# Attention scores in quarters of the TensorE array, in an attention and token-mixing kernel

## The chip, the cores and the metric

The kernel runs on one core of a Trainium2 chip. The metric is the device time of one execution in microseconds (us), as the median over runs. A core has TensorE (PE, matrix products into PSUM; its weight loads are listed apart as PEld), VectorE (DVE), ScalarE (ACT), GpSimd (POOL) and SyncE (SP), which run beside one another and wait for each other by semaphores.

## The reference

Attention with a local window and a few global keys, then a mixing layer on its output. Cut to what is computed:

```python
B, H, S, D = 4, 8, 768, 64;  n_global, n_local = 8, 96
scores = q @ k.T / sqrt(D)                        # per batch and head, 768 x 768
keep   = (key < n_global) | (0 <= query - key < n_local)
scores = where(keep, scores - slope[h] * dist, -1e9)   # dist: query - key, or n_local for global keys
a      = softmax(scores);   attn = a @ v
x      = attn with the heads side by side         # B, 768, 512
theta  = x @ w_theta
y      = w_tok_r @ (x * cos(theta)) + w_tok_i @ (x * sin(theta))
u      = x + y
out    = u + relu(u @ w_ch)                       # f32
```

## The kernel before

All matrix operands are bf16 and sums are f32. Queries and keys are cut into six tiles of 128 (T). Because the window is 96 and there are 8 global keys, a query tile needs its own key tile and the one before it; the first 8 keys of the earlier tile are replaced by the global ones in a second copy of the keys (`mT`, and `v_pv` for the values). Eleven blocks of 128 keys by 128 queries are left per head. They lie in three groups (`GROUPS`): group 0 with three blocks, groups 1 and 2 with four each. A group of two heads fills one `ps_w` tile of PSUM, two banks, one for each head; there are two such tiles.

Heads go in pairs (`h0` = 0, 2, 4, 6). `att_transpose` turns q and k of two heads so that the 64 channels lie in the partitions: head `h0` in partitions 0 to 63, head `h0 + 1` in 64 to 127. For batches 1 to 3 that is done by 48 transposes of 64 by 64 (L226), and two copies bring the result from PSUM to the tile `qk` (L232, both on ScalarE in the steps spoken of here). `att_scores` (L297) then makes one matmul per block and head: the stationary operand (weights) is a block of keys, 64 channels by 128 keys, in the upper or the lower half of the array's rows according to the head; the moving operand is the queries' 128 columns (256 where one key block serves two query tiles, in group 0). The weights of each matmul are loaded by an instruction of their own. ScalarE takes the exponential (L306), VectorE multiplies by a mask with the slopes in it (L317, L319), and `att_values` (L346) multiplies by the values, which also yields the sums of the softmax.

In batch 0 the bias is added in PSUM for groups 0 and 2: `att_bias` (L276) writes a product that covers the bank, and the scores add to it (L302 takes the exponential). In the other batches the scores start the sum themselves.

The program is written in the order in which each engine runs it (`K` keeps the program order). In batches 1 to 3 the attention of a batch runs beside the mixing of the batch before (`attend_beside`): for every two heads the order on PE is group 0's scores, some matmuls of the mixing (L430 with `w_tokT`, L472 with `w_ch`), the scores of groups 1 and 2, the transposes of the next two heads, more mixing, and the values. Between batches come the matmuls with `w_theta` (L395) with sine and cosine on ScalarE (L403, L404). Loads are issued by POOL, results and transposing DMAs by SP.

Of the kernel before, what the change touches and what calls it, by code (L numbers as in the profile page):

```python
# [16 lines left out]
def kernel(  # L17
# [13 lines left out]
    nc = tc.nc  # L31
    B, H, S, D = q.shape
    T = 128
# [20 lines left out]
    K = tc.keep_in_program_order  # L54

    def ps_wide():
        return psum.tile([T, 2, DM], FP, name="ps_w", tag="ps_w", bufs=2)
# [208 lines left out]
    def att_bias(h0, g_):  # L266

        ps = biased[h0, g_] = ps_wide()
        rows = dist.rearrange("a n t -> a (n t)")
        for hh in range(2):  # L270
            if g_ == 0:
                out_, rhs = ps[:, hh, 0:3 * T], rows
            else:
                out_ = ps[:, hh, :].rearrange("a (r x) -> a r x", r=2)
                rhs = rows[:, None, T:3 * T].to_broadcast([T, 2, 2 * T])
            K(nc.tensor.matmul(out_, lhsT=ident_d[:, h0 + hh, :], rhs=rhs,  # L276
                               start=True, stop=False))

    def att_scores(b, h0, g_, mul=True):
        qT, kT, mT = qTs[b, h0], kTs[b, h0], mTs[b, h0]  # L280
        blocks = GROUPS[g_]
        n = len(blocks)
        bias = b == 0 and g_ != 1
        if bias and (h0, g_) not in biased:
            att_bias(h0, g_)
        ps = biased[h0, g_] if bias else ps_wide()

        runs = [(0, 2)] + [(2, 1)] if g_ == 0 else [(i_, 1) for i_ in range(n)]
        for i_, w in runs:
            it, prev = blocks[i_]  # L290
            if prev == 0 or it == 1:
                keys = kT[:, (it - prev) * T:(it - prev + 1) * T]
            else:
                keys = mT[:, (it - 2) * T:(it - 1) * T]
            for hh in range(2):
                R = slice(D * hh, D * (hh + 1))
                K(nc.tensor.matmul(ps[:, hh, i_ * T:(i_ + w) * T],  # L297
                                   lhsT=keys[R, :], rhs=qT[R, it * T:(it + w) * T],
                                   start=not bias, stop=not bias or i_ == n - 1))
        if bias:  # L300
            p = abuf.tile([T, 2, 4 * T], BF, name="p", bufs=6)
            K(nc.scalar.activation(p[:, :, 0:n * T], ps[:, :, 0:n * T], AF.Exp, scale=scale))  # L302
            probs[b, h0, g_] = p
            return
        e = abuf.tile([T, 2, 4 * T], BF, name="e", bufs=3)
        K(nc.scalar.activation(e[:, :, 0:n * T], ps[:, :, 0:n * T], AF.Exp, scale=scale))  # L306
        exps[b, h0, g_] = e
        if mul:
            att_mul(b, h0, g_)

    def att_mul(b, h0, g_):
        e = exps[b, h0, g_]
        n = len(GROUPS[g_])
        p = abuf.tile([T, 2, 4 * T], BF, name="p", bufs=6)
        hs = slice(h0, h0 + 2)
        if g_ == 0:
            K(nc.vector.tensor_mul(p[:, :, 0:n * T], e[:, :, 0:n * T], wmask[:, hs, :]))  # L317
        else:
            K(nc.vector.tensor_mul(  # L319
                p.rearrange("a h (r x) -> a h r x", r=2),  # L320
                e.rearrange("a h (r x) -> a h r x", r=2),
                wmask[:, hs, None, T:3 * T].to_broadcast([T, 2, 2, 2 * T])))
        probs[b, h0, g_] = p
# [179 lines left out]
    def attend_beside(b, main, lead, load):  # L503


        def m(n=1):
            for _ in range(n):
                main.pop(0)()

        m(lead)  # L510
        for h0 in range(0, H, 2):
            att_scores(b, h0, 0)
            m(2 if h0 else 1)
            att_scores(b, h0, 1)
            att_scores(b, h0, 2)
            if h0 + 2 < H:
                att_transpose(b, h0 + 2, q_eng="act")
                if load and h0 == 0:
                    load_heads(b + 1, 0, 4)
                if load and h0 + 4 == H:  # L520
                    load_heads(b + 1, 4, 4)
                m(2)
            else:
                if load:
                    turn_x(b, NC - 2, False)
                m(len(main) - 1)
            att_values(b, h0)
            if h0 + 2 < H and not (load and h0 + 4 == H):
                turn_x(b, h0 // 2, True)
        m()  # L530
# [136 lines left out]
```

## Time and profile before

| | |
|---|---|
| Time, median of 3 runs | 171.58 us (171.09 to 172.12) |
| Profiled execution | 171.33 us, span 169.5 us |
| Granted TensorE clock | 1.000 |
| Busy: PE / PEld / DVE / ACT / POOL | 158.7 / 86.2 / 114.7 / 103.0 / 63.2 us |
| Score matmuls (L297) | 288 with 128 columns, 32 with 256 |
| Transposes in quarters (L226) | 576 |

The span is from the first to the last instruction of the program in one profiled execution; the time of the run is 1.8 us longer. A group's row gives the line, the engine, the operation with its output and inputs by name, the used rows*columns of the array (for PE), the shape and the count; then busy time, mean duration, and the idle time of the engine before it with what ended it. Matmuls overlap: one of 128 columns is listed with some 216 ns, while the next starts 56 ns later. So for PE the distances between starts tell more than durations. A few matmul records are missing from the trace (276 of 288 rows of L430 are there).

### The profile page before, as it was taken

The numbers are of one execution on the slowest core, as the hardware profiler recorded it, in microseconds if no ns is written. First come the engines' busy times: TensorE is split into PE (matmuls) and PEld (weight loads), VectorE is DVE, ScalarE is ACT, GpSimd is POOL, SyncE is SP. The second block draws the span as 40 slices with busy tenths as digits, with TensorE's granted clock in tenths as the row PEclk, the third lists the DMA queues.
The fourth block names the chain that finished last, engine by engine and source line by source line (L and its number), as shares of the span: only waits on it lengthen the run. The fifth ranks groups of instructions, "written<-read, shape, count | busy, mean of one in ns | idle before, by whom it ended". The sixth has DMA issues, their size and how long they took to land.

```text
span 169.5 us, 4624 instructions
## 1 busy us (share of the span) xinstructions
PE 158.7 (94%) x1965; PEld 86.2 (51%) x1988; DVE 114.7 (68%) x210; ACT 103.0 (61%) x120; POOL 63.2 (37%) x99
## 2 busy tenths in 40 slices
PE   7779999999899999999999999999999999999992
PEld 2346665555465654446555554445655544444440
DVE  7768875965858875767587694849568756534362
ACT  4989887957686562798658615996765618300010
POOL 8996797004484650032972900054245000000000
PEclk9999999999999999999999999999999999999999
DMA  4999999999999999910599999711953342121325
GB/s 148 194 180 190 209 211 208 198 180 182 158 140 196 141 173 215 257 70 4 92 145 170 155 187 197 210 62 37 73 110 95 99 148 86 68 60 34 113 102 186
DMA packets 57060, 24.08 MB, mean 142 GB/s; under 512 B 43088, under 2 KB 54096, under 8 KB 57040
## 3 DMA queue, kind: packets, MB, share of 16 engines
q0 software_dynamic: 35328, 12.45, 65.5%
q1 hardware_dynamic: 21440, 10.95, 31.2%
q10 hardware_dynamic: 272, 0.39, 0.7%
q8 instruction: 15, 0.25, 0.6%
q14 instruction: 5, 0.04, 0.1%
HBM read 25.69 MB, written 6.29 MB: 189 GB/s over the span
## 4 chain that ended last, share of the span: by engine, by line
PE 80%; DVE 6%; DMA 4%; issue 3%; POOL 3%; ACT 3%; DVEq 0%; ACTq 0%; POOLq 0%
PE ps_mm L430 35%; PE ps_mm L472 12%; PE ps_w L395 11%; PE ps_w L297 7%; PE ps_w L346 5%; DMA v_sb<-in_v_dram 4%; PE ps_tr L226 3%; PE ps_mm L346 2%; ACT e L306 2%; PE ps_tr L114 2%; DVE zri L411 1%; DVE w_tokT L117 1%; PE ps_tr L378 1%; DVE p L319 1%; ACT qk L249 1%
## 5 line engine op out<-in xcount | busy, mean ns | idle before, releaser
L430 PE MATMUL ps_mm<-zri,w_tokT 128*128 128x512 bf16 x276 | 67.0, 380 | 1.3 <-issue 0.8
L306 ACT ACTIVATE e<-ps_w 128x1024 bf16<-128x1024 f32 (+1 forms) x40 | 37.1, 958 | 17.8 <-PE ps_w L297 17.8
L430 PEld LDWEIGHTS <-w_tokT 128*128 128x128 bf16 x288 | 26.2, 98 | 30.3 <-issue 2.3
L257 POOL COPY qk<-qk 128x512 bf16<-128x512 bf16 x15 | 9.5, 636 | 65.2 <-ACT qk L232 53.0
L319 DVE TENSOR_TENSOR p<-e,wmask 128x1024 bf16<-128x1024 bf16 x28 | 19.9, 712 | 11.8 <-ACT e L306 11.8
L403 ACT ACTIVATE cs<-ps_w,halfpi 128x1024 bf16<-128x1024 f32 x12 | 13.4, 1116 | 18.6 <-PE ps_w L395 18.6
L435 DVE TENSOR_TENSOR u<-x_sb,ps_mm 128x512 bf16<-128x512 bf16 x24 | 16.2, 683 | 12.2 <-PE ps_mm L430 12.2
L395 PE MATMUL ps_w<-w_theta_bf,xT 128*128 128x512 bf16 x91 | 22.6, 379 | 0.6 <-ACT cs L404 0.3
L411 DVE TENSOR_TENSOR zri<-cs,x_sb 128x1024 bf16<-128x1024 bf16 x24 | 16.1, 688 | 9.1 <-ACT cs L403 7.7
L472 PE MATMUL ps_mm<-w_ch_bf,uTd 128*128 128x512 bf16 x82 | 21.5, 379 | 0.6 <-issue 0.5
L297 PE MATMUL ps_w<-qk 64*128 64x128 bf16 (+1 forms) x320 | 16.1, 223 | 2.3 <-DVE qk L249 0.8
L475 DVE SCALAR_TENSOR_TENSOR o_sb<-ps_mm,u 128x512 f32<-128x512 f32 (+2 forms) x25 | 16.5, 664 | 1.1 <-PE ps_mm L472 0.9
L232 ACT COPY qk<-ps_tr 128x768 bf16<-128x768 bf16 x21 | 16.0, 815 | 2.0 <-issue 2.0
L297 PEld LDWEIGHTS <-qk 64*128 64x128 bf16 x320 | 10.0, 94 | 12.1 <-issue 7.8
L346 PEld LDWEIGHTS <-p 128*128 128x128 bf16 x352 | 13.2, 97 | 4.6 <-DVE p L319 0.8
L395 PEld LDWEIGHTS <-xT 128*128 128x128 bf16 x96 | 9.0, 98 | 10.8 <-issue 0.5
L80 POOL DMA_DIRECT2D v_sb<-in_v_dram x10 | 13.0, 1299 | 0.0
L472 PEld LDWEIGHTS <-uTd 128*128 128x128 bf16 x88 | 8.2, 98 | 9.0 <-issue 0.2
L404 ACT ACTIVATE cs<-ps_w 128x1024 bf16<-128x1024 f32 x12 | 12.2, 1020 | 0.0
L92 POOL COPY v_pv<-v_sb 8x520 bf16<-8x520 bf16 x15 | 11.5, 767 | 0.9
L354 DVE TENSOR_TENSOR x_sb<-ps_w,rec 128x768 bf16<-128x768 f32 x12 | 11.5, 958 | 0.4
L346 PE MATMUL ps_w<-v_sb,p 128*128 128x65 bf16 x168 | 11.3, 193 | 0.0
(84 smaller groups left out, 180.2 us busy)
## 6 DMA issues: line engine op xcount, KB each, us to landing
out_dram<-o_sb SPq DMA_DIRECT2D x23, 256.0 KB, 2.3
q_sb<-in_q_dram POOLq DMA_DIRECT2D x6, 384.0 KB, 6.2
k_sb<-in_k_dram POOLq DMA_DIRECT2D x6, 384.0 KB, 9.0
v_sb<-in_v_dram POOLq DMA_DIRECT2D x6, 384.0 KB, 13.5
w_nat<-in_moe_w_tok_r_dram POOLq DMA_DIRECT2D x1, 1152.0 KB, 12.3
w_nat<-in_moe_w_tok_i_dram POOLq DMA_DIRECT2D x1, 1152.0 KB, 13.4
v_sb<-in_v_dram POOLq DMA_DIRECT2D x4, 192.0 KB, 6.7
q_sb<-in_q_dram POOLq DMA_DIRECT2D x3, 192.0 KB, 5.9
```

The costliest lines, as they stand in the source:

```text
L232: K(op(out=qk[:, 0:2 * S].rearrange("a (i r p t) -> a i r p t", i=2, r=2, t=NT)[:, :, r, :, :], in_=halves[r].rearrange("a (i t p) -> a i ...
L297: K(nc.tensor.matmul(ps[:, hh, i_ * T:(i_ + w) * T], lhsT=keys[R, :], rhs=qT[R, it * T:(it + w) * T], start=not bias, stop=not bias or i_ ...
L306: K(nc.scalar.activation(e[:, :, 0:n * T], ps[:, :, 0:n * T], AF.Exp, scale=scale))
L319: K(nc.vector.tensor_mul(p.rearrange("a h (r x) -> a h r x", r=2), e.rearrange("a h (r x) -> a h r x", r=2), wmask[:, hs, None, T:3 * T].t ...
L346: K(nc.tensor.matmul(dst, lhsT=lhsT, rhs=rhs, start=(i_ == 0), stop=(i_ == len(mms) - 1)))
L395: K(nc.tensor.matmul(pth[:, s2, :], lhsT=xTs[b][:, dc, c:c + T], rhs=w_theta_bf[:, dc, :], start=(dc == 0), stop=(dc == NC - 1)))
L403: K(nc.scalar.activation(cs[:, :, 0, :], pth, AF.Sin, bias=halfpi))
L411: K(nc.vector.tensor_mul(zris[b][:, st:st + 2, wi, :].rearrange("a s (c d) -> a s c d", d=T), cs[:, :, wi, :].rearrange("a s (c d) -> a s ...
L430: K(nc.tensor.matmul(acc, lhsT=w_tokT[wi][:, st, tt * T:(tt + 1) * T], rhs=zris[b][:, st, wi, :], start=(done[b, tt] == 0), stop=(done[b, ...
L435: K(nc.vector.tensor_add(us[b][:, tt, :].rearrange("a (c d) -> a c d", d=T), x_sb[b][:, :, tt, :], acc.rearrange("a (c d) -> a c d", d=T)))
L472: K(nc.tensor.matmul(pc[:, 0:N], lhsT=uT[:, c:c + T], rhs=w_ch_bf[:, dc, cols], start=(dc == 0), stop=(dc == NC - 1)))
L475: K(nc.vector.scalar_tensor_tensor(o_sb, in0=pc[:, 0:N], scalar=0.0, in1=us[b][:, tt, cols], op0=ALU.max, op1=ALU.add))
```

## The change

Each score matmul is cut in two by keys. The weights are 64 channels by 64 keys, and the product goes to the lower or the upper 64 partitions of the same PSUM tile. For one key block there are now four products in a row: two heads (rows 0 to 63 and 64 to 127 of the array) by two halves of the keys (columns 0 to 63 and 64 to 127). The queries that stream through are the same 128 or 256 columns for both halves. It holds for all batches, with and without the bias in PSUM. Everything else is the same; the lines after the change are three further down.

```diff
             for hh in range(2):
                 R = slice(D * hh, D * (hh + 1))
-                K(nc.tensor.matmul(ps[:, hh, i_ * T:(i_ + w) * T],
-                                   lhsT=keys[R, :], rhs=qT[R, it * T:(it + w) * T],
-                                   start=not bias, stop=not bias or i_ == n - 1))
+                for c in range(2):
+                    C = slice(D * c, D * (c + 1))
+                    K(nc.tensor.matmul(ps[C, hh, i_ * T:(i_ + w) * T],
+                                       lhsT=keys[R, C], rhs=qT[R, it * T:(it + w) * T],
+                                       start=not bias, stop=not bias or i_ == n - 1))
```

## The prediction

> **What bounds the kernel now.** I read the page from the top: the busy shares, then the chain of work that ended last, then the costliest groups, and from there the timeline of one attention step.
>
> ```profile
> span 169.5 us, 4624 instructions
> PE 158.7 (94%) x1965; PEld 86.2 (51%) x1988; DVE 114.7 (68%) x210; ACT 103.0 (61%) x120; POOL 63.2 (37%) x99
> ...
> PE 80%; DVE 6%; DMA 4%; issue 3%; POOL 3%; ACT 3%; DVEq 0%; ACTq 0%; POOLq 0%
> ...
> L306 ACT ACTIVATE e<-ps_w 128x1024 bf16<-128x1024 f32 (+1 forms) x40 | 37.1, 958 | 17.8 <-PE ps_w L297 17.8
> L297 PE MATMUL ps_w<-qk 64*128 64x128 bf16 (+1 forms) x320 | 16.1, 223 | 2.3 <-DVE qk L249 0.8
> ```
>
> TensorE (PE) is busy 94% of the span and holds 80% of the chain; the score matmuls of L297 are 320 instructions. A single average says "PE-bound", so every nanosecond saved on PE would seem to count. But the ACT row has 17.8 us of idle time ended by these very score matmuls, so ACT and PE may be taking turns. The timeline decides it. First PE, from the second score stretch of a step (groups 1 and 2, 16 matmuls) into the transposes of the next two heads:
>
> ```profile
> 82.06 0.38 PE L430 MATMUL ps_mm<-zri,w_tokT 128*128 128x512 bf16 x1
> 82.37 0.62 PE L297 MATMUL ps_w<-qk 64*128 64x128 bf16 x16
> 82.92 0.22 PE L226 MATMUL ps_tr<-ident,k_sb 64*64 64x64 bf16 x4
> 82.97 0.20 PE L226 MATMUL ps_tr<-ident,q_sb 64*64 64x64 bf16 x4
> 83.00 0.20 PE L226 MATMUL ps_tr<-ident,k_sb 64*64 64x64 bf16 x4
> 83.03 0.20 PE L226 MATMUL ps_tr<-ident,q_sb 64*64 64x64 bf16 x4
> ```
>
> Columns: start, duration, engine, line, operation, used part of the array (rows*columns), shape, count. Two things are to be seen. The 16 score matmuls of 64*128 start from 82.37 to 82.77 (two start within 3 ns of each other, one head in each half of the array's rows; the next two 56 ns later). And the transposes of L226 already run in quarters, 64*64, four at a time, a new four every 0.03 us (32 ns between starts in this stretch, 3 to 4 ns within a four). So this trace shows what four quarter products with four weight loads cost, for 64 columns. Between the last score matmul (82.77) and the first transpose (82.92) lie 146 ns, where neighbours of one shape follow after 56 ns (a 128-column transpose of L378 and the matmul after it): changing the shape in use costs about 90 ns.
>
> Then ACT in the same step:
>
> ```profile
> 82.81 1.94 ACT L306 ACTIVATE e<-ps_w 128x1024 bf16<-128x1024 f32 x2 [1.36 <-PE ps_w L297]
> 84.63 1.51 ACT L232 COPY qk<-ps_tr 128x768 bf16<-128x768 bf16 x2
> 86.57 0.81 ACT L306 ACTIVATE e<-ps_w 128x768 bf16<-128x768 f32 x1 [0.43 <-PE ps_w L297]
> ```
>
> and PE at the end of that step:
>
> ```profile
> 85.35 0.19 PE L346 MATMUL ps_w<-v_sb,p 128*128 128x65 bf16 x1
> 85.53 0.20 PE L346 MATMUL ps_w<-v_pv,p 128*128 128x65 bf16 x1
> ...
> 85.96 0.19 PE L346 MATMUL ps_w<-v_sb,p 128*128 128x65 bf16 x1
> 86.08 0.22 PEld L297 LDWEIGHTS <-qk 64*128 64x128 bf16 x4
> ...
> 86.19 0.34 PE L297 MATMUL ps_w<-qk 64*128 64x256 bf16 x4
> ```
>
> From the end of group 1's scores ACT works without a gap: two exponentials, then the two copies of the next heads' q and k, to 86.14. The next step's first score matmul starts at 86.19, 50 ns after the copy, with its weights loaded at 86.08 and waiting. I compared all nine places where scores follow values: the score matmul starts 50 ns after the last copy's end in every one. A second wait lies earlier in the same stretch: the value matmuls pause from 85.35 to 85.53 (29 ns apart elsewhere) for the second probability tile, which VectorE makes from ACT's second exponential. So a step is a loop: scores of group 0 and 1 with eight L430 matmuls between them on PE (86.19 to about 88.7), then 3.3 us of ACT. PE's group 2 scores, transposes and values lie beside ACT, with about 0.10 us to spare at the end and 0.15 us in the pause. The chain does not show this, since waits this short are lost between long rows.
>
> **The change part by part.** Every score matmul of 64 rows by 128 keys becomes two of 64 by 64; PE issues 320 matmuls and 320 weight loads more, in the same places; the other engines' instructions, all DMAs and the number of PE's waits are the same. No step is moved past a queue.
>
> 1. *Streaming.* Two heads by 128 keys become two heads by two halves of 64 keys, four products abreast, over the same 128 (or 256) columns. Products that ran two abreast already used all 128 rows and 128 columns, so there is no array time to win: 56 ns a pair now. For a four the nearest row is the transposes' 32 ns for 64 columns, where single matmuls of 65 columns (L346) come every 29 ns: 3 ns more for a four. In those fours the next weights are issued about 2 ns after a four and its matmul starts 30 ns later, so I take the weights as what sets 32 ns; for 128 columns 56 ns cover that. I take 0; the upper bound is the same ratio, 32/29 of 56, or 8 ns a four for 128 columns read generously (twice 32).
>
> 2. *Start of a group.* After a change of shape the first matmuls wait for their weights: the first 128-column pair records 226 ns against 216 later, the first four of transposes 213 against 193. So 20 ns instead of 10: +10 ns. The last of four starts about 10 ns after the first, the last of two 3: +7 ns, felt by ACT and by the next shape. Together 17 ns per group that starts on the path; bounds 0 and, if both the change into and out of the shape pay, 25.
>
> 3. *The 90 ns before the transposes go,* in the nine steps (three a batch, batches 1 to 3) where they follow scores: 9 x 0.09 = 0.8 us of PE time. The next thing late is ACT: the transposes would end 90 ns earlier, the value matmuls arrive 90 ns earlier at the pause that ends with the second probability tile, and what they don't lose there they lose at the copy. Both are counted from the end of group 1's scores. I take 0; bounds 0 and -0.8.
>
> On the path, then: group 0 and group 1 of 12 steps, 2 x 17 ns x 12 = 0.41 us; in batch 0 the chain has four pieces of L297 at 12.10, 16.47, 20.75 and 22.35, 4 x 17 = 0.07 us. Sum +0.48, say +0.5 us. The profiled execution took 171.33 us (span 169.5 and 1.8 around it) and would take 171.8; it lies 0.25 below the median of 171.58, so by the median 172.1, 0.3% more.
>
> [...] The rows above show four weight loads and four matmuls issued 3 to 4 ns apart although two of each four share their rows. [...]
>
> **The rivals.**
>
> *The saved 0.8 us passes (171.3).* If the two waits were not ACT's, part 3 would count: 171.58 + 0.5 - 0.8. For it: the chain runs through PE there, and all nine changes of shape are in it. Against it: 50 ns after the copy, nine times of nine.
>
> *Fours stream slower than pairs (173.0, slower).* The 3 ns that a four of transposes costs over a single matmul grows with the columns: 8 ns per 128. On the path a step has 7 times 128 columns of fours (group 0: 2 + 1, group 1: 4), 12 steps 84, batch 0 about 18, and group 2 of the last step in batches 2 and 3, where the values wait for nothing, 8: 110 x 8 = 0.9 us, with the 0.5 above 1.4. It decides (0.5% is 0.86 us) from 0.36 / 110, some 3 ns per four, on. For it: a four carries twice the instructions and twice the moving streams of a pair. Against it: weights explain the 32 ns.
>
> *Quarters of the same rows follow one another (about 178).* Each four takes two turns, 56 ns more: 110 x 56 = 6.2 us, with 0.5 about 178; group 2's extra 0.22 us of the other steps disappears in the waits above. For it: scores differ from transposes (f32 sums, both quarters read the same queries). Against it: the transposes' fours.
>
> **How the numbers follow.** About 0.5% is what a measurement here can tell from no change (the three runs before spread from 171.09 to 172.12), so "same" reaches from 170.7 to 172.4. The forecast, +0.5 us, has 0.60, of which 0.09 ends above 172.4 (a four 3 ns slower, or 25 ns a group) and 0.01 below; the saved time passing 0.12, of which 0.03 lies below 170.7 (when part 2 costs nothing either); slower fours 0.18; quarters in turn 0.07; 0.03 for what I don't see, spread over the three. Faster 0.05, same 0.60, slower 0.35. The range reaches down to 170.9 (saved time passes, part 2 nearly free) and up to 173.1 (slower fours); the turn-taking case is left out. The likeliest case's own range is 171.6 to 172.6.
>
> **What the profile afterwards would show.** Right: score rows as 64*64 with 640 matmuls, four starting within 10 ns, fours of 128 columns 56 to 58 ns apart; first transpose about 56 ns after a score four instead of 146; a longer pause in the values or before group 0's scores, still 50 ns after the copy; the step from one group 0 to the next (5.93 us now, 80.26 to 86.19) longer by some 35 ns. Wrong: steps shorter than 5.93 us (the gain passes), fours 60 ns apart or more (slower fours), or a fresh wait before scores that neither ACT nor POOL ends.

## The result

The changed kernel takes 173.07 us (median of 8 runs, 172.27 to 173.89) against 171.83 us for the kernel before on the same chips: ratio 1.0077, interval 1.0050 to 1.0103. It is slower by 1.2 us, where the prediction had 0.5 us, within what it called "same". The profiled execution took 172.91 us, 1.58 more than the one of before. Ratios here and below leave out executions that took over 1.5% more than the fastest of their kernel, among them four of twelve in a2, two of twelve in c1 and one each in a3, b1, b2 and b4.

From the page of the changed kernel, in the order of the lines shown of before:

```profile
span 171.1 us, 5287 instructions
PE 161.2 (94%) x2308; PEld 87.3 (51%) x2308; DVE 114.5 (67%) x210; ACT 103.0 (60%) x120; POOL 62.9 (37%) x99
...
PE 74%; DVE 8%; ACT 6%; DMA 4%; issue 3%; POOL 3%; DVEq 0%; ACTq 0%; POOLq 0%
...
L309 ACT ACTIVATE e<-ps_w 128x1024 bf16<-128x1024 f32 (+1 forms) x40 | 37.1, 958 | 19.3 <-PE ps_w L300 19.3
...
L300 PE MATMUL ps_w<-qk 64*64 64x128 bf16 (+1 forms) x640 | 17.0, 226 | 3.0 <-DVE qk L258 0.8
```

640 score matmuls, all 64*64. ACT's work is the same to 0.1 us, its idle time before the exponentials grew from 17.8 to 19.3 us, and the chain gives PE 74% instead of 80%, ACT and VectorE more. So the share of the span that the chain lays on PE became smaller.

The same step as before, in the timeline of PE and then of ACT:

```profile
82.66 0.64 PE L300 MATMUL ps_w<-qk 64*64 64x128 bf16 x32
83.14 0.20 PE L226 MATMUL ps_tr<-ident,k_sb 64*64 64x64 bf16 x4
83.16 0.20 PE L226 MATMUL ps_tr<-ident,q_sb 64*64 64x64 bf16 x4
```

```profile
83.13 1.94 ACT L309 ACTIVATE e<-ps_w 128x1024 bf16<-128x1024 f32 x2 [1.37 <-PE ps_w L300]
84.96 1.51 ACT L232 COPY qk<-ps_tr 128x768 bf16<-128x768 bf16 x2
86.92 0.81 ACT L309 ACTIVATE e<-ps_w 128x768 bf16<-128x768 f32 x1 [0.46 <-PE ps_w L300]
```

```profile
85.57 0.19 PE L349 MATMUL ps_w<-v_sb,p 128*128 128x65 bf16 x1
85.85 0.20 PE L349 MATMUL ps_w<-v_pv,p 128*128 128x65 bf16 x1
...
86.41 0.25 PEld L300 LDWEIGHTS <-qk 64*64 64x64 bf16 x8
86.52 0.36 PE L300 MATMUL ps_w<-qk 64*64 64x256 bf16 x8
```

The eight fours of groups 1 and 2 start at 82.66, 82.74 and then every 56 ns. The first transpose starts 46 ns after the last score matmul (146 before). And the next step's group 0 starts at 86.52, 51 ns after ACT's copies end (86.47), with the load of its weights started at 86.41. The 0.1 us that vanished before the transposes is gone into the pause in the values: it grew from 0.18 us (85.35 to 85.53 before) to 0.28 us (85.57 to 85.85). The wait at the copy did not change: from the weight load to the first score it is 98 to 106 ns before and 101 to 106 ns after, and in all nine places the scores still start 50 to 51 ns after the copy.

Steps and stretches show where the time came from. The stretches run from a batch's first score matmul to the next batch's, and from batch 3's to the end of the span. Microseconds, read from the trace; "no wait" is the run a3 below:

| | a step (6 of them) | batch 1 | batch 2 | batch 3 and rest |
|---|---|---|---|---|
| before | 5.930 | 35.73 | 36.33 | 58.01 |
| before, again (a1) | 5.930 | 35.73 | 36.33 | 58.00 |
| changed | 5.976 | 35.89 | 37.52 | 58.19 |
| changed, again (a2) | 5.976 | 35.89 | 37.06 | 58.20 |
| changed, no wait (a3) | 5.976 | 35.91 | 36.50 | 58.21 |

Each of these six steps, the second and third of a batch, is 46 ns longer: 15 ns from group 0 to group 1, 31 ns from group 1 to the next group 0. The first step of a batch has one unit of mixing less; it grew by 30 to 50 ns (from 4.995, 5.062 and 5.063 us to 5.025, 5.112 and 5.113). Over the three stretches, without the waits that follow, the growth is 0.16, 0.18 and 0.19 us; with 0.07 in batch 0 it is 0.6 us. Batch 2 holds something else. In the timeline of the changed kernel, PE and then its weight loads:

```profile
92.49 0.36 PE L300 MATMUL ps_w<-qk 64*64 64x256 bf16 x7
93.46 0.24 PE L300 MATMUL ps_w<-qk 64*64 64x128 bf16 x1 [0.61 <-issue]
93.63 0.39 PE L433 MATMUL ps_mm<-zri,w_tokT 128*128 128x512 bf16 x1
```

```profile
92.39 0.24 PEld L300 LDWEIGHTS <-qk 64*64 64x64 bf16 x7
93.46 0.10 PEld L300 LDWEIGHTS <-qk 64*64 64x64 bf16 x1 [0.82 <-issue]
```

Between the seventh and the eighth of eight equal products, in a batch whose operands are all there, PE stands still for 0.82 us, and nothing in the profile ends it ("issue"). Group 1's scores start 0.85 us late for it. No such wait stands in the profiles of before. A third, smaller part is a transfer: the first matmul of L475 after 104.08 waits some 0.17 us for a transposed tile (`uTd`). 0.6 + 0.85 + 0.17 is the 1.6 us by which this execution's span grew.

### The profile page after: what moved, and what is told of

Its sections match the earlier page's. It is cut to its first block, busy times and chain, and to the rows that moved or that the text cites. A ratio compares the mean times of both kernels' runs of the same rounds, so it can differ in the third digit from the quotient of the medians.

```text
span 171.1 us, 5287 instructions
## 1 busy us (share of the span) xinstructions
PE 161.2 (94%) x2308; PEld 87.3 (51%) x2308; DVE 114.5 (67%) x210; ACT 103.0 (60%) x120; POOL 62.9 (37%) x99
## 4 chain that ended last, share of the span: by engine, by line
PE 74%; DVE 8%; ACT 6%; DMA 4%; issue 3%; POOL 3%; DVEq 0%; ACTq 0%; POOLq 0%
PE ps_mm L433 30%; PE ps_w L398 11%; PE ps_mm L475 11%; PE ps_w L300 7%; ACT e L309 5%; PE ps_w L349 5%; DMA v_sb<-in_v_dram 4%; DVE p L322 4%; PE ps_tr L226 3%; DVE w_tokT L117 2%; PE ps_mm L349 2%; PE ps_tr L114 1%; DVE zri L414 1%; PE ps_tr L381 1%; ACT qk L249 1%
## 5 line engine op out<-in xcount | busy, mean ns | idle before, releaser
L433 PE MATMUL ps_mm<-zri,w_tokT 128*128 128x512 bf16 x288 | 68.7, 380 | 0.1
L309 ACT ACTIVATE e<-ps_w 128x1024 bf16<-128x1024 f32 (+1 forms) x40 | 37.1, 958 | 19.3 <-PE ps_w L300 19.3
L475 PE MATMUL ps_mm<-w_ch_bf,uTd 128*128 128x512 bf16 x88 | 22.5, 379 | 0.0
L300 PE MATMUL ps_w<-qk 64*64 64x128 bf16 (+1 forms) x640 | 17.0, 226 | 3.0 <-DVE qk L258 0.8
L300 PEld LDWEIGHTS <-qk 64*64 64x64 bf16 x640 | 11.4, 106 | 12.8 <-issue 8.6
L475 PEld LDWEIGHTS <-uTd 128*128 128x128 bf16 x88 | 8.1, 98 | 9.3 <-DMA uTd<-u 0.8
L357 DVE TENSOR_TENSOR x_sb<-ps_w,rec 128x768 bf16<-128x768 f32 x12 | 11.5, 957 | 0.4
```

Source lines behind the costliest of these rows:

```text
L300: K(nc.tensor.matmul(ps[C, hh, i_ * T:(i_ + w) * T], lhsT=keys[R, C], rhs=qT[R, it * T:(it + w) * T], start=not bias, stop=not bias or i_ ...
L433: K(nc.tensor.matmul(acc, lhsT=w_tokT[wi][:, st, tt * T:(tt + 1) * T], rhs=zris[b][:, st, wi, :], start=(done[b, tt] == 0), stop=(done[b, ...
L475: K(nc.tensor.matmul(pc[:, 0:N], lhsT=uT[:, c:c + T], rhs=w_ch_bf[:, dc, cols], start=(dc == 0), stop=(dc == NC - 1)))
```

## The experiments

Theory A at the start: the 46 ns a step are the cost of quarters at the start of groups that lie on the path, ACT absorbs the gain, and the long wait is PE waiting for its own instructions, because the stream is longer. Theory B: the wait is an accident of one execution.

**a1, a2: both kernels again.** No edit.

> The kernel before, once more, as the yardstick. All theories: ratio 1.000 within 0.003, group 0 to group 0 in a step 5.93 us (80.26 to 86.19 in the first trace), no wait of PE inside a group of scores that nothing in the profile ends. If the 0.6 us wait of the changed kernel (92.85 to 93.46, in the middle of a group of scores, with 'issue' as its end) is an accident of any run, one like it may stand here too.

> The changed kernel, once more. Theory A (two costs): the steps are each 46 ns longer again (31 ns from group 0 to group 1, 15 ns from group 1 to the next group 0), in all 0.7 us, and on top comes a wait of PE for its own instructions, which recurs because the instruction stream is longer (18 fetches of the instruction queue against 15): ratio 1.007, a wait of 0.3 to 1 us near the same place. Theory B (the wait was an accident of one execution): the same 0.7 us in the steps, no such wait, ratio 1.004.

Measured: 0.9993 (0.9970 to 1.0015) for before; 1.0056 (1.0023 to 1.0090) for the changed kernel. The steps repeat to the nanosecond. The wait is there again, before the same eighth weight load, 0.33 us long (92.63 to 92.96). It is no accident of one execution. (The expectation has the two parts of the 46 ns the wrong way round: the 15 come first, the 31 after.)

**a3: the same instructions, 64 places later.**

```diff
-    keep_warm(8)
+    keep_warm(5)
+    small = ps_acc()
+    for _ in range(35):
+        K(nc.tensor.matmul(small[:, 0:64], lhsT=zero[:, 0:T], rhs=zero[:, 0:64],
+                           start=True, stop=True))
```

> The changed kernel with 35 matmuls of 64 columns in place of 3 of 512 among the warm-up matmuls at the start, where PE waits for the first loads anyway: all later instructions of PE stand 64 places later in its stream. Theory A (PE waits for a block of instructions): the wait, if there, comes 64 instructions earlier in the program's terms, that is among the last value matmuls before that group of scores instead of at its eighth weight load, or is gone because the fetch falls differently; ratio between 1.004 and 1.008. Theory B (accident): no relation with the place, ratio 1.004.

Measured: 1.0046 (1.0015 to 1.0077). No such wait anywhere, steps of 5.976 us, batch 2 in 36.50 us. So 0.18 us in batch 2 is the quarters, and the wait of 0.82 and 0.33 us that the other two executions have beyond that depends on where the instructions lie. Their wait of 0.2 us for a transposed tile is gone here too.

**a4: as many instructions, in the old shape.** Score matmuls cut by queries:

```diff
+            W = w * T // 2
+            for c in range(2):
-            for hh in range(2):
+                for hh in range(2):
-                K(nc.tensor.matmul(ps[:, hh, i_ * T:(i_ + w) * T],
-                                   lhsT=keys[R, :], rhs=qT[R, it * T:(it + w) * T],
+                    K(nc.tensor.matmul(ps[:, hh, i_ * T + c * W:i_ * T + (c + 1) * W],
+                                       lhsT=keys[R, :],
+                                       rhs=qT[R, it * T + c * W:it * T + (c + 1) * W],
...
```

> The kernel before, with each score matmul cut by queries instead of by keys: the same 640 matmuls and weight loads as the changed kernel, but all of them 64*128 as before, so no change of the shape, no four abreast, and the 90 ns before the transposes stay. Theory A (instruction stream): as many fetches as in the changed kernel, the same kind of wait, and about 3 ns a pair (two times 29 against 56) at 110 pairs on the path, 0.3 us: ratio 1.004 to 1.007. Theory B: 0.3 us alone, ratio 1.002. The 31 and 15 ns a step, if they are due to quarters, are not here; a few ns take their place.

Measured: 1.0034 (1.0001 to 1.0066), and in its timeline:

```profile
91.88 0.37 PE L299 MATMUL ps_w<-qk 64*128 64x128 bf16 x7
92.89 0.20 PE L299 MATMUL ps_w<-qk 64*128 64x64 bf16 x1 [0.64 <-issue]
```

The wait stands before the same place of the stream, 0.83 us long, without a single quarter. So quarters as such don't make it: it came with the same number of instructions in the old shape. The steps surprised: 5.89 us, 40 ns shorter than before. Its first two products of group 0 (one for each head) start 47 ns before ACT's second copy ends; the next two follow from 51 ns after that end. (The cut was meant to cost 3 ns a pair. It does within group 1, where ACT begins 450 instead of 439 ns after the first product, 11 ns for four pairs, and it gains more at the start.)

**b1, b2: take ACT's pace away.** One unit of mixing from ahead of group 1 to behind the transposes, with pairs (b1) and with quarters (b2):

```diff
-            m(2 if h0 else 1)
+            m(1)
...
-                m(2)
+                m(3 if h0 else 2)
```

> Pairs as before; in the steps of the second, third and fourth head pair one unit of mixing (four matmuls of 512 columns, 0.86 us) is moved on PE from between group 0 and group 1 to behind the transposes, beside ScalarE. Theory A (a step is scores of groups 0 and 1 on PE followed by 3.33 us of ScalarE, and PE waits about 0.25 us a step for it): in the steps of heads 2 and 4 PE no longer waits, 5.93 becomes about 5.68 us, six times 0.25 plus about 0.3 us in the last step of batch 1: about 1.8 us less, ratio 0.990. Rival (PE sets the step, the waits are noise): ratio 1.000.

> The same move with quarters. Theory A: where ScalarE no longer sets the step, the 90 ns that vanish before the transposes count, against some 45 ns that the quarters cost on PE in a step: the steps of heads 2 and 4 are 40 to 50 ns shorter than with pairs and the same move, those of head 0 still 46 ns longer; together 0 to 0.2 us less than pairs with the move, apart from waits for instructions (up to 0.8 us). Rival (the quarters cost on PE itself, whoever waits): 46 ns a step more here too, 0.7 us more than pairs with the move.

Measured: 1.0331 (1.0299 to 1.0364) and 1.0360 (1.0323 to 1.0396). As a whole the expectation failed. PE, in the kernel with pairs:

```profile
91.57 1.03 PE L472 MATMUL ps_mm<-w_ch_bf,uTd 128*128 128x512 bf16 x4
93.39 0.59 PE L430 MATMUL ps_mm<-zri,w_tokT 128*128 128x512 bf16 x2 [0.79 <-DVE u L435]
```

The moved unit's next matmul waited 0.79 us for VectorE to empty a PSUM tile (L435, 92.65 to 93.33). VectorE's work there stands behind the two probability tiles (L319), for which it had waited 0.94 and 0.22 us for ACT's exponentials. PE also waited 2.5 us for a transposed tile for L472. But single steps answer the question. Steps in which neither happened: 5.671 and 5.675 us in batch 1 with pairs (5.68 was expected), 5.872 and 5.868 in batches 2 and 3; with quarters the latter two are 5.783 and 5.784. So with ACT's pace taken away quarters make a step 84 to 89 ns shorter, and with it 46 ns longer. That is more than the 40 to 50 ns expected, and the trace shows why: in these two steps group 2's scores start 53 to 54 ns after VectorE has emptied their PSUM tile (L354, L357 with quarters), 1.66 us after group 0's with pairs and with quarters alike. What the quarters cost ahead of that point is hidden in this wait, and the gain behind it remains. (Batch 1's steps with quarters contain waits of the kind above, 1.24 and 0.60 us.)

**b3, b4: quarters in some groups only.** In the changed kernel's loop, with `(2,)` for b3 and `(0, 1)` for b4:

```diff
-                for c in range(2):
-                    C = slice(D * c, D * (c + 1))
+                for C in ([slice(0, D), slice(D, T)] if g_ in (2,) else [slice(0, T)]):
```

> Quarters in group 2 alone, pairs in groups 0 and 1. Theory A: group 2 lies beside ScalarE, so the step stays at 5.93 us to a few ns; the change of shape now lies between groups 1 and 2 instead of before the transposes; 256 instructions more on PE; ratio 1.000 to 1.001, unless a fetch of instructions falls badly (up to 0.8 us). Rival (quarters cost in proportion to their number): 8 of the 20 matmuls of a head pair are cut, 0.3 us, ratio 1.002, with steps 18 ns longer.

> Quarters in groups 0 and 1, pairs in group 2. Theory A: the whole cost is here: the step 46 ns longer (15 ns from group 0 to group 1, 31 ns after), 0.7 us, ratio 1.004, plus what a badly placed fetch of instructions may add (384 instructions more on PE). Rival (in proportion): 12 of 20 cut, 28 ns a step, ratio 1.0025.

Measured: b3 1.0024 (1.0003 to 1.0045), b4 1.0070 (1.0043 to 1.0096). PE's timeline of b3:

```profile
86.62 0.34 PE L299 MATMUL ps_w<-qk 64*128 64x256 bf16 x4
88.73 0.74 PE L299 MATMUL ps_w<-qk 64*128 64x128 bf16 x24
...
92.55 0.34 PE L299 MATMUL ps_w<-qk 64*128 64x256 bf16 x4
```

With quarters in group 2 alone the six steps are 5.930 us and the first ones 4.998, 5.063 and 5.063, as before: 8 of 20 products cut, and nothing to pay. Batches 2 and 3 grew by 0.14 (without 0.16 that PE waited for a transposed tile) and 0.15 us: in their last step the values wait for nothing, so nothing hides what group 2 costs, and the change of shape from group 1 to group 2 is an extra one. (In batch 1's last step the values do pause; there the pause shrinks from 0.35 to 0.22 us and the stretch stays as it was.) With quarters in groups 0 and 1 the steps that nothing disturbs are 5.976 to 5.978 us. All of the 46 ns lie in the groups ahead of ACT's work; a cost in proportion (18 and 28 ns) is ruled out. The profiled execution of b4 took 175.22 us against a median of 172.57 for the other five: PE stood still in it three times without a named cause (0.65, 0.39 and 0.94 us) and waited 1.6 us for a transposed tile.

These places lead further. Leaving aside waits of at most 0.2 us ahead of L430 and L472, of which the trace of the kernel before shows eight, PE stands still without a named cause in six of the profiled executions so far and below (the changed kernel twice, a4, b2, b4 and c1). Counted in PE's stream of weight loads and matmuls, the places are 3007 in the changed kernel twice, in a4 and in c1; 1471 in the second run of the changed kernel; 1471 and 1727 in b2; 1215, 1727 and 2751 in b4. All are multiples of 256 apart, to within one place. The page also has the packets of the instruction queue, q8. Its row before and after the change:

```profile
q8 instruction: 15, 0.25, 0.6%
q8 instruction: 18, 0.29, 0.7%
```

These are 15 and 18 packets of 16 KB. In all of the places above the last one starts 2.3 to 3.3 us ahead of the instruction that PE waits for. At place 3007 it starts when PE has begun its 2943rd instruction, 64 earlier. So I formed theory C: PE gets its instructions in blocks of 256, and waits where a block runs out within some 2.3 to 3.3 us of the next block's fetch. It is drawn from the distance of 256 between the waits and from the count, three packets more for 640 instructions more; no row tells what a packet holds. The time alone does not tell where a wait comes: places that lie a multiple of 256 from these were also passed without one 2.26 us (place 703 of the changed kernel) and 2.91 us (place 447 of the kernel before) after the start of a packet.

The 64 of place 3007 does not repeat: in b2 and b4 the fetch starts 38 to 146 places ahead of the wait, and in d1 below 48.

**c1, c2: is the fetch late because of other transfers?** Both kernels without one load:

```diff
         load_qk(b, h0, n)
-        load_v(b, h0, n)
+        if (b, h0) != (B - 1, 0):
+            load_v(b, h0, n)
```

> The changed kernel without one load: the values of the first four heads of batch 3 (384 KB as bf16, issued by GpSimd at 84.2 in the earlier profiles) are not loaded, so the outputs of those heads in that batch are made from older values; all engine work is the same. Theory A (the block of PE's instructions arrives late because its transfer stands behind these loads): the fetch that started at 90.5, 434 instructions after its predecessor, starts earlier, the wait of 0.3 to 0.8 us at place 3007 of PE's stream is gone, the stretch from batch 1's to batch 2's first scores takes 36.50 us as in the shifted kernel instead of 37.06 to 37.52; ratio 1.004. Rival (the place in the stream alone decides, whatever the other transfers do): the wait stays at place 3007, ratio 1.006 to 1.008.

> The kernel before without the same load, as the yardstick of the run above. Both theories: 35.73, 36.33 and 58.0 us for the three stretches between the batches' first scores and the end, as before: ratio 1.000.

Measured: c1 1.0054 (1.0027 to 1.0081), c2 0.9979 (0.9962 to 0.9996). In c1 the wait stays before the same weight load, 0.75 us (92.85 to 93.60), the fetch starts at the same place of the stream, and the transposed tile comes 1.05 us late. Theory A's part on the loads falls: these loads don't make this fetch late. They do take part elsewhere: without them the fetch that follows starts 100 instructions earlier, at place 3020 instead of 3120 in the changed kernel, and the one that starts at place 2864 in the kernel before starts at 2764 in c2. In time the fetch follows PE: it starts at 90.55, 90.53, 90.92 and, in a4 with its shorter steps, at 89.97, at the same instruction each time (to the few records that are missing).

**c3: use the 40 ns of a4.** Pairs, group 0's matmul of 256 queries cut into two of 128:

```diff
+            for c in range(w):
-            for hh in range(2):
+                for hh in range(2):
-                K(nc.tensor.matmul(ps[:, hh, i_ * T:(i_ + w) * T],
-                                   lhsT=keys[R, :], rhs=qT[R, it * T:(it + w) * T],
+                    K(nc.tensor.matmul(ps[:, hh, (i_ + c) * T:(i_ + c + 1) * T],
+                                       lhsT=keys[R, :],
+                                       rhs=qT[R, (it + c) * T:(it + c + 1) * T],
...
```

> Pairs of 64*128 as before, only that in group 0 the matmul of 256 queries is cut into two of 128 (32 matmuls and weight loads more in all). With all matmuls cut by queries the first matmul of group 0 had started before ScalarE's second copy was done, and the steps were 40 ns shorter. Theory A (a step is group 0 and 1 on PE after ScalarE's last copy): the first two products move ahead of the copy's end, steps about 5.88 us instead of 5.93, nine times 50 ns: 0.4 us less, ratio 0.997. Rival (the 40 ns came from the finer cut of group 1): steps of 5.93, ratio 1.000.

Measured: 0.9997 (0.9972 to 1.0023). Steps of 5.87 to 5.88 us, as expected, and 0.17 and 0.15 us less in the first and third stretch. The ratio of 0.997 that was expected did not come: the second stretch took 37.49 us instead of 36.33:

```profile
101.67 1.24 PE L397 MATMUL ps_w<-w_theta_bf,xT 128*128 128x512 bf16 x5
104.06 1.04 PE L474 MATMUL ps_mm<-w_ch_bf,uTd 128*128 128x512 bf16 x4 [1.15 <-DMA uTd<-u]
```

That tile was issued at 94.75 and landed at 104.01. In the kernel before it was issued at 95.05 and landed at 102.76, and PE used it at 102.83 without a wait: the kernel before stands at the edge there. From 85 to 106 its transfer engines are busy 90% of the time or more in every slice of the page. So this edit shortens the steps, and no gain of the kernel is shown.

**d1: does the wait follow the block or the work?** As a3, with 16 instructions more instead of 64:

```diff
-    keep_warm(8)
+    keep_warm(7)
+    small = ps_acc()
+    for _ in range(9):
...
```

> The changed kernel with 16 instructions more among PE's warm-up matmuls (9 of 64 columns in place of 1 of 512). Theory C (PE gets its instructions in blocks of 256, with an end of a block at the stream's places 1215, 1471, 1727, 2751 and 3007, where waits have been seen; a wait comes where a block is used up within 2.4 to 2.9 us of the next fetch): the wait stays at place 3007 of the stream, which is now the last value matmul before that group of scores instead of the group's last weight load; the other stretches as in the changed kernel; ratio 1.004 to 1.008. Rival (the wait belongs to the last scores of that group, whatever its place): it stays at the group's last weight load.

Measured: 1.0109 (1.0071 to 1.0148). PE, and its weight loads:

```profile
93.33 0.19 PE L353 MATMUL ps_w<-v_pv,p 128*128 128x65 bf16 x1
94.26 0.20 PE L353 MATMUL ps_w<-v_sb,p 128*128 128x65 bf16 x1 [0.73 <-issue]
94.39 0.36 PE L304 MATMUL ps_w<-qk 64*64 64x256 bf16 x8
```

```profile
94.25 0.10 PEld L353 LDWEIGHTS <-p 128*128 128x128 bf16 x1 [0.85 <-issue]
94.39 0.14 PEld L304 LDWEIGHTS <-qk 64*64 64x64 bf16 x8
```

The wait left the scores and stands before the last value matmul: place 3007, where theory C had put it. The fetch ahead of it starts at the same instruction of the program as in the changed kernel, now 48 places ahead of the wait. Sixteen cheap instructions among the warm-up matmuls, 90 us earlier, moved a wait of 0.9 us; 64 removed it in the profiled run. The rest of what d1's profiled execution has beyond the quarters' 0.6 us are two waits for transposed tiles (0.65 us at 67.2, 0.24 at 105.1) and a later start: the second head pair's scores of batch 0 begin at 12.52 instead of 12.10, as they do in c2, where in a1 it is 11.89. So the ratio of 1.0109 is not the price of the moved wait.

## Why the prediction was wrong

*What bounds the kernel: right.* The step is scores of groups 0 and 1 on PE, then ACT: exponentials and copies keep their distances to the nanosecond (921, 904 and 1508 ns), and scores start 50 ns after the copy in both kernels. b3 and b4 show which groups count.

*Streaming (part 1): right.* Fours come every 56 ns for 128 columns, 0 more than pairs. The rival of slower fours falls. So does that of quarters in turn: two quarters of the same rows start 3 to 4 ns apart.

*Start of a group (part 2): right in kind, too small.* 34 ns a step were forecast, 46 measured. From group 0 to group 1 it is 15 ns (17 forecast); from group 1 on 31, of which 14 are the first four (80 ns instead of 66 to the next), 7 the later start of the last product, and 9 that ACT begins 267 instead of 258 ns after that start. The last was not in the sum. On the path it comes to 0.6 us instead of 0.48.

*The 90 ns before the transposes (part 3): right.* They vanished, the pause in the values grew by as much (0.18 to 0.28 us), and the step gained nothing, since ACT sets it; b2 shows them passing, 84 to 89 ns a step, where it does not. The rival of the passing gain falls for this kernel.

*The sum: wrong, and here the prediction failed.* It was made from array time, and 320 matmuls and weight loads more were entered "in the same places" at no cost of their own, without naming what supplies them; "the number of PE's waits" was to stay the same. It did not: PE stood still for 0.82 and 0.33 us at place 3007 of its stream, by theory C for its own instructions. In a4, with as many instructions and without any quarter, it stood still for 0.83 us at the same place. In the profiled execution the wait was 0.85 of 1.6 us, the steps 0.6 and a transposed tile 0.17. The prediction's own list of signs had this one: "a fresh wait before scores that neither ACT nor POOL ends". Where the wait does not occur in the profile (a3) the ratio is 1.0046, close to the 0.35% that the steps' 0.6 us come to. But the changed kernel itself gave 1.0077 and 1.0056, and the intervals of these three overlap, so the ratios alone do not price the wait. The time of 173.07 lies at the very end of the stated range, and only the case of slower fours, which is not what happened, had carried it that far.

Two things stay open. What decides when a packet of the instruction queue starts: in the changed kernel that is 15 to 241 places after the last place that lies a multiple of 256 from 3007, but ahead of place 3007 it is the same instruction in the changed kernel twice, in a4 and in c1; the loads left out in c1 don't set it there but move the next packet by 100 places, and other transfers were not tried. And how much of each median is this wait: the profiles show single executions, and the waits for transposed tiles (0.2 to 1.5 us) vary too.

## What to carry to other kernels

Cutting an instruction in two can cost more than engine time (here 640 instructions more on PE came with a wait of 0.33 to 0.83 us, with quarters and without, though not in the shifted kernel): look for a wait ended by "issue" in the middle of equal work, and count its place in the engine's stream. Before costing a saving on the busiest engine, find the row that waits a constant time for another engine (here 50 ns after a copy, nine times of nine): what was saved before it, 90 ns a step, was lost in it, and what was added ahead of the other engine's work, 46 ns a step, was paid in full. And 16 cheap instructions moved a wait of 0.9 us that came 90 us later, so a kernel at such an edge is to be compared with a shifted copy of itself.

## What the runs showed of the hardware

- PE's waits without a named cause that the kernel before does not have (0.33 to 1.24 us where their length is given above) lie a multiple of 256 instructions of its stream apart (places 1215, 1471, 1727, 2751, 3007), and end 2.3 to 3.3 us after the start of a 16 KB packet of the instruction queue. They keep to the place in the stream and not to the work (d1).
- Four products of 64*64 with their own weights run abreast at the pace of two of 64*128: 56 ns for 128 columns, starts 3 to 4 ns apart; only the first four after a change of shape is slower, 80 ns to the next against 66 for pairs.
- A change of the shape in use costs about 90 to 100 ns between matmuls: from scores to transposes it is 146 ns, with one shape 46; from group 1 to group 2 in b3 it is 146, where pairs follow after 52.
